# Attention taken in natural tile order, low weights in one transfer per chunk, small softmax steps on ACT, late weights over two superblocks

## The chip, the cores and the metric

The kernel runs on one core of a Trainium2 chip. The time is that of one execution on the device, in microseconds (us). The engines are TensorE (PE; PEld is its weight load), VectorE (DVE), ScalarE (ACT), GpSimd (POOL) and SyncE (SP), which here issues nearly all transfers. Each engine runs its own queue of instructions in order; engines wait for one another by semaphores.

## The reference

Three layers follow one another; `x` between them has 4608 tokens of 512 values.

```python
# attention, q, k, v: 8 batches x 8 heads x 576 x 64, in chunks of 64 positions
scores = scale * np.matmul(q_c, k_c.transpose(0, 1, 2, 4, 3))
scores = scores - np.max(scores, axis=-1, keepdims=True)
attn = np.exp(scores)
attn = attn / (np.sum(attn, axis=-1, keepdims=True) + 1e-09)
out = np.matmul(attn, v_c)
# layer 1 and layer 2 (512 -> 1536 -> 512); layer 2 takes xn
g = x @ w_gate
silu = g * (1.0 / (1.0 + np.exp(-g)))
val = x @ w_val
return (silu * val @ w_out).astype(np.float32)
# ahead of layer 2
rms = np.sqrt(np.mean(x * x, axis=-1, keepdims=True) + 1e-06)
xn = x / rms * rms_g
```

The weights come as float64 and are used to float32 accuracy.

## The kernel before

**Arithmetic.** Every float32 operand of a large product is split into a high part in a reduced type and a low part, and each product is three matmuls (`mm3`, L570 to L572): high x high, low x high, high x low. A weight thus exists as a high tile (kept on the chip) and a low tile.

**Stages of layer 1.** Seven blocks of 512 tokens (numbered 0 to 6), each in 12 chunks of the hidden size; a chunk has 36 matmuls of 128x512: 12 for g, 12 for v, 12 for y of the chunk before. Block 0 (26 to 143 us of the trace, "the head") also turns the float64 weights into high and low parts on ACT and VectorE: L124, L125, L135, L140, and `to_lo` (L158), which computes a low tile; `keep` (L1271) stores it to `lo_scratch` five conversions later. From block 1 on (143 us) `load_lo` (L179, transfer at L182) loads the low tiles of g, v and o of a chunk, two chunks ahead, into three sets of buffers. Between the blocks' matmuls stand, one attention tile (128 tokens) every 6.75 positions with three positions to a chunk: 28 tiles (8 to 35) lie in blocks 1 to 5, so each block has 5 or 6 of them and block 6 has none. `load_qk` and `load_v` make lists of transfers for groups of five chunks of 64 tokens; `issue` (L376, L378) issues them on SyncE, a few at a time.

**Attention tile.** `trans_att` transposes q and k, TensorE computes the scores (L406), `att_m` takes the maximum on VectorE (L426), scales it on POOL (L429), and ACT makes the exponentials `p` and their sums `r` (L434); `att_n` adds 1e-9 to `r` on POOL (L454), VectorE inverts it (L463), POOL multiplies (L464), VectorE transposes (`att_td`, L480), and TensorE multiplies with v (L522). Which tokens tile i has is set by `order`: the layers' blocks hold natural token ranges, and tiles 28 to 35 (the last 1024 tokens) are taken in between others.

**Work beside it in blocks 0 to 5.** Weights of layer 2 are converted, combined (`comb_add`, L210) and split (`comb_split`, L216 to L218) on ACT and POOL and stored to `w_scratch`. For the last 1024 tokens layer 1 uses seven combined products per 2x2 blocks in place of eight, and its combined weights are made here: `whole` (L226, plain parts stored at L230), `first_add` (L245), `first_keep` (L248), with two buffers `wa`. All of these are placed by `put` at positions of blocks.

**Superblocks.** Superblock 0 (1043 to 1267 us) is layer 1 for the last 1024 tokens: 504 matmuls for g and v, 252 for y. Its combined weights come back from `w_scratch` whole and are split here by `ring_split` (ACT copy L870, POOL subtraction L871; 72 of them); the norm of block 6 (`rms_*`) and four late output weights of layer 2 (`late_o`, for fp 2 to 5) are placed among its matmuls by `late`. Superblocks 1 to 5 (1267 to 2057 us) are layer 2; in superblock 1 lies the norm of the last tokens (`norm`).

## Time and profile before

| | us |
|---|---|
| median of 3 runs | 2056.97 (2056.14 to 2058.54) |
| profiled execution | 2057.85 |
| its span in the trace | 2056.1 |

| engine | busy in us | share of the span |
|---|---|---|
| TensorE matmuls | 1795.0 | 87% |
| weight loads | 1485.1 | 72% |
| VectorE | 1283.3 | 62% |
| ACT | 802.3 | 39% |
| POOL | 607.6 | 30% |

The busy shares are a mean over stages with different limits, so they don't say what ends a stage. The trace is read by stage: a window gives the busy time of each engine in a stretch; a list of waits names who waited for whom; the chain goes back from the last instruction to what released it; the timeline gives single events. SyncE's issues are no busy time of an engine, but they take time in its queue and stand in the chain as SPq. All times below are from the one profiled execution.

### The profile page before, as it was taken

To read this page: it belongs to the slowest core of one execution; us is meant where nothing else is said; L and a number is where in the kernel's file an instruction comes from. 1 tells how busy PE (TensorE), PEld (TensorE's weight loads), DVE (VectorE), ACT (ScalarE), POOL (GpSimd) and SP (SyncE) were. 2 spreads that over 40 slices of the span, in tenths; PEclk is the share of its full clock that TensorE was granted. 3 is DMA by queue.
4 is the path that set the end of the run, shared out by engine and by line. 5 is a ranking of instruction groups with operands and counts; after the bars stand their busy time and mean duration, and the time that the engine had idled before them with its cause. 6 is when DMAs were issued, how large, how long until landed. Compare 5 with 4: busy or idle time off the path is not lost.

```text
span 2056.1 us, 30283 instructions
## 1 busy us (share of the span) xinstructions
PE 1795.0 (87%) x9978; PEld 1485.1 (72%) x9978; DVE 1283.3 (62%) x2208; ACT 802.3 (39%) x1846; POOL 607.6 (30%) x641
## 2 busy tenths in 40 slices
PE   7996587788476696799988899999999999999998
PEld 5875365566354575578876677778888888899998
DVE  7964265465254465576565596679558747758657
ACT  6751233332132142343344464335235334435333
POOL 1003245333444443453164665302001101101100
PEclk9998799899787898899999999999999999999999
DMA  9964455645554465663556636676876876797986
GB/s 246 299 167 114 116 169 156 178 137 141 140 161 139 108 192 160 171 192 114 159 168 201 219 114 191 181 243 198 251 214 182 267 209 189 212 321 223 325 252 188
DMA packets 489355, 391.11 MB, mean 190 GB/s; under 512 B 285424, under 2 KB 355312, under 8 KB 489200
## 3 DMA queue, kind: packets, MB, share of 16 engines
q1 hardware_dynamic: 487600, 388.99, 64.9%
q8 instruction: 80, 1.31, 0.3%
q14 instruction: 75, 0.61, 0.1%
q10 hardware_dynamic: 1600, 0.20, 0.1%
HBM read 309.07 MB, written 79.95 MB: 189 GB/s over the span
## 4 chain that ended last, share of the span: by engine, by line
PE 49%; SPq 13%; DVE 10%; DMA 10%; POOL 7%; issue 7%; ACT 3%; POOLq 0%; ACTq 0%; DVEq 0%
SPq L378 10%; DMA lo<-lo_scratch 2%; PE g L570 1%; DVE hp L1047 1%; PE g L571 1%; PE ygA L571 1%; PE g L572 1%; PE yvA L570 1%; PE yvA L572 1%; PE ygA L572 1%; PE yvA L571 1%; PE ygA L570 1%; ACT p L434 1%; DVE pT L480 1%; PE v L570 1%
## 5 line engine op out<-in xcount | busy, mean ns | idle before, releaser
L1011 POOL TENSOR_TENSOR h<-h,h 128x512 f32<-128x512 f32 (+1 forms) x36 | 46.4, 1290 | 510.6 <-DVE h L989 509.8
L572 PE MATMUL g<-xh,lg 128*128 128x512 f32 x336 | 139.6, 415 | 40.7 <-DMA lg<-lo_scratch 40.6
L570 PE MATMUL g<-xh,wg 128*128 128x512 f32 x336 | 140.8, 419 | 27.4 <-DVE sg L583 25.7
L1047 DVE TENSOR_TENSOR hp<-h,hp 128x512 fp32r<-128x512 f32 (+1 forms) x216 | 151.0, 728 | 6.6 <-ACT hp L1046 6.3
L570 PE MATMUL v<-xh,wv 128*128 128x512 f32 x336 | 135.4, 403 | 19.9 <-DVE sg L599 16.7
L480 DVE STREAM_TRANSPOSE pT<-p 32x128 f32<-32x128 f32 x448 | 135.6, 303 | 16.3 <-POOL p L464 10.1
L1046 ACT CAST hp<-h 128x512 fp32r<-128x512 f32 (+1 forms) x216 | 121.9, 584 | 57.3 <-PE yvA L572 21.0
L570 PE MATMUL y<-hh,wo 128*128 128x512 f32 x168 | 73.8, 439 | 76.8 <-ACT hh L602 76.8
L571 PE MATMUL g<-xl,wg 128*128 128x512 f32 x336 | 137.7, 410 | 0.4 <-DVE xl L564 0.4
L969 ACT ACTIVATE sig<-sgt 128x512 f32<-128x512 f32 (+1 forms) x108 | 64.5, 597 | 175.6 <-DVE sgt L977 175.6
L970 DVE TENSOR_TENSOR sgt<-sgt,sig 128x512 f32<-128x512 f32 (+1 forms) x108 | 72.3, 669 | 96.2 <-ACT sig L969 96.2
L571 PE MATMUL v<-xl,wv 128*128 128x512 f32 x336 | 132.0, 393 | 0.0
L572 PE MATMUL v<-xh,lv 128*128 128x512 f32 x336 | 131.8, 392 | 0.0
L908 POOL TENSOR_TENSOR xf<-xf,xf 128x512 f32<-128x512 f32 (+1 forms) x48 | 80.0, 1666 | 156.7 <-DMA wro<-w_scratch 94.8
L602 ACT CAST hh<-sg 128x512 fp32r<-128x512 f32 x84 | 52.4, 624 | 149.2 <-DVE sg L599 149.1
L572 PEld LDWEIGHTS g<-xh,lg 128*128 128x128 f32 x336 | 67.4, 201 | 59.7 <-DMA lg<-lo_scratch 44.5
L463 DVE RECIPROCAL r<-r 128x8 f32<-128x8 f32 x36 | 7.3, 203 | 153.1 <-POOL r L454 152.9
L570 PEld LDWEIGHTS g<-xh,wg 128*128 128x128 f32 x336 | 67.4, 200 | 48.3 <-DVE sg L583 32.0
L571 PE MATMUL y<-hl,wo 128*128 128x512 f32 x168 | 74.6, 444 | 30.2 <-DVE hl L604 29.9
L434 ACT ACTIVATE p<-both,m 128x64 f32<-128x64 f32 x224 | 66.9, 327 | 81.9 <-POOL m L429 81.9
L570 PEld LDWEIGHTS y<-hh,wo 128*128 128x128 f32 x168 | 34.1, 203 | 88.3 <-ACT hh L602 81.3
L583 DVE SCALAR_TENSOR_TENSOR sg<-sg,g 128x512 f32<-128x512 f32 x84 | 56.8, 676 | 56.8 <-ACT sg L582 56.4
(859 smaller groups left out, 5454.3 us busy)
## 6 DMA issues: line engine op xcount, KB each, us to landing
wrg<-w_scratch SPq DMA_DIRECT2D x210, 256.0 KB, 3.3
wrv<-w_scratch SPq DMA_DIRECT2D x210, 256.0 KB, 3.3
wro<-w_scratch SPq DMA_DIRECT2D x210, 256.0 KB, 3.1
lg<-lo_scratch SPq DMA_DIRECT2D x54, 256.0 KB, 3.0
lv<-lo_scratch SPq DMA_DIRECT2D x54, 256.0 KB, 3.4
lo<-lo_scratch SPq DMA_DIRECT2D x54, 256.0 KB, 3.7
w_scratch<-wsg SPq DMA_DIRECT2D x42, 256.0 KB, 2.4
w_scratch<-wsv SPq DMA_DIRECT2D x42, 256.0 KB, 2.3
```

Of the source, the lines that this page charges most:

```text
L378: nc.sync.dma_start(out=o, in_=i)
L434: nc.scalar.activation(pt[:, hp, x], s3[:, x, hp], AF.Exp, scale=SCALE, bias=m[:, x, hp:hp + 1], accum_out=r[:, 2 * hp + x],)
L480: nc.vector.transpose(out=pT[o:o + 32, :, r:r + 32], in_=pt[r:r + 32, :, z, b * 32:b * 32 + 32])
L570: nc.tensor.matmul(o, sh, mh, start=first, stop=False, skip_group_check=free)
L571: nc.tensor.matmul(o, sh, ml, start=False, stop=False, skip_group_check=free)
L572: nc.tensor.matmul(o, sl, mh, start=False, stop=last, skip_group_check=free)
L583: return sg, lambda: nc.vector.scalar_tensor_tensor(out=sg[:, :n], in0=sg[:, :n], scalar=1.0, in1=g[:, :n], op0=ALU.add, op1=ALU.mult)
L908: nc.gpsimd.tensor_sub(o, a, b)
L969: nc.scalar.activation(sg[:, :tw], src[:, :tw], AF.Sigmoid)
L970: nc.vector.tensor_mul(t[:, :tw], src[:, :tw], sg[:, :tw])
L1046: nc.scalar.copy(hh[:, :tw], src)
L1047: nc.vector.tensor_sub(hl[:, :tw], src, hh[:, :tw].bitcast(F32))
```

## The change

- **Order and storage.** Attention tiles go through the tokens in natural order. Which columns of the layers' storage a tile takes is set by `home` and `order`: tiles 33, 34, 35, 12, 13, 22, 23 and 24 are the last 1024 columns. A group of five chunks is then a continuous range, except where a batch ends, so its q and k come in fewer, wider transfers: 832 before, 544 after. Stores of the result follow `rows`: 172 in place of 156, the 16 more in the last superblock.
- **Low weights.** The low tiles of g, v and o of a chunk are one tile and one transfer of 768 KB (L184 of the new kernel), 54 in place of 162. The tile's buffer is released when its last reader is done.
- **Stores of combined weights** go in pairs: 72 in place of 126.
- **Small softmax steps.** The scaling of the maximum (L449) and the 1e-9 (L456) are ACT's for tiles 8 to 35; POOL's two are gone.
- **`ring_split`.** VectorE subtracts 34 of the 72 and the low halves of the others stay on POOL.
- **Late weights.** `late_o` for fp 2 and 3 stays in superblock 0, at positions 30 and 50; for fp 4 and 5 it goes to superblock 1, at positions 3 and 23.

SyncE's transfers in the two programs, counted in the order of its queue from the load of a chunk's low weights to the next (chunks 3 to 10 one by one; the last number is chunk 11 with chunks 0 to 2 of the next block):

| block | before | after |
|---|---|---|
| 1 | 22, 48, 44, 24, 18, 7, 3, 7, 99: 272 | 10, 31, 28, 18, 14, 4, 1, 5, 61: 172 |
| 2 | 28, 34, 22, 18, 10, 7, 3, 35, 83: 240 | 26, 31, 20, 15, 7, 4, 1, 18, 51: 173 |
| 3 | 52, 50, 12, 14, 11, 8, 24, 37, 101: 309 | 21, 19, 8, 11, 7, 5, 20, 34, 65: 190 |
| 4 | 49, 22, 13, 9, 8, 14, 33, 37, 88: 273 | 20, 12, 9, 6, 6, 12, 29, 34, 55: 183 |
| 5 | 21, 13, 5, 9, 8, 19, 19, 14, 24: 132 | 14, 10, 2, 6, 6, 16, 16, 11, 19: 100 |

SyncE, block 1, from the low weights of the sixth chunk (index 5) to those of the seventh; `x3` and `x4` are like transfers in a row. Before:

```order
L182 DMA lg_1_5_2221<-lo_scratch 128x512
L182 DMA lv_1_5_2223<-lo_scratch 128x512
L182 DMA lo_1_5_2225<-lo_scratch 128x512
L378 DMA xk_2123<-in_k_dram 32x6x32 x3
L378 DMA xk_2123<-in_k_dram 32x2x32 x4
L378 DMA xq_2122<-in_q_dram 32x2x32 x4
L378 DMA xq_2122<-in_q_dram 32x6x32 x4
L378 DMA xq_2122<-in_q_dram 32x2x32 x4
L378 DMA xk_2123<-in_k_dram 32x2x32 x4
L378 DMA xk_2123<-in_k_dram 32x6x32 x4
L378 DMA xk_2123<-in_k_dram 32x2x32 x4
L378 DMA xq_2122<-in_q_dram 32x2x32 x4
L378 DMA xq_2122<-in_q_dram 32x6x32 x4
L378 DMA xq_2122<-in_q_dram 32x2x32 x2
L182 DMA lg_1_6_2344<-lo_scratch 128x512
```

After:

```order
L184 DMA l_1_5_2140<-lo_scratch 128x1536
L398 DMA xk_2057<-in_k_dram 32x4x32
L398 DMA xk_2057<-in_k_dram 32x6x32 x4
L398 DMA xq_2056<-in_q_dram 32x4x32 x4
L398 DMA xq_2056<-in_q_dram 32x6x32 x4
L398 DMA xk_2057<-in_k_dram 32x4x32 x4
L398 DMA xk_2057<-in_k_dram 32x6x32 x4
L398 DMA xq_2056<-in_q_dram 32x4x32 x4
L398 DMA xq_2056<-in_q_dram 32x6x32 x2
L184 DMA l_1_6_2245<-lo_scratch 128x1536
```

Between the loads of low weights stood 41 transfers of q and k pieces, most of them 2 wide, and now 27 of 4 and 6; the low weights are one row in place of three.

POOL, end of block 3, where the weights of chunk 10 are made whole (`wav`, third tile in two buffers). Before:

```order
L429 TENSOR_SCALAR m_5969<-m_5969 128x8
L226 TENSOR_TENSOR wav_5986<-wv_0_520,lv_3_10_5676 128x512
L245 TENSOR_TENSOR wav_5845<-wav_5845 128x256
L454 TENSOR_SCALAR r_5972<-r_5972 128x8
L464 TENSOR_TENSOR p_5970<-p_5970,r_5972 128x512
```

After:

```order
L228 TENSOR_TENSOR wav_5631<-wv_0_518,l_3_10_5330 128x512
L248 TENSOR_TENSOR wav_5491<-wav_5491 128x256
L480 TENSOR_TENSOR p_5614<-p_5614,r_5616 128x512
L228 TENSOR_TENSOR wav_5711<-wv_0_447,l_3_11_5449 128x512
L248 TENSOR_TENSOR wav_5631<-wav_5631 128x256
```

The small steps on `m` and `r` are gone from the row; `p` still comes after `wav`.

ACT at the scores of tile 24 (`both` is the scores, `wsv` a layer-2 weight, `hh` the hidden values of block 4, chunk 0). Before:

```order
L538 COPY x_23_6167<-both_6134 128x2x4x64
L434 ACTIVATE p_6211,r_6213<-both_6134,m_6210 128x64 x8
L216 CAST wsv_3_6237<-wtv_3_6185 128x256
L602 CAST hh_4_0_6207<-sg_4_0_6132 128x512
```

After:

```order
L554 COPY x_23_5808<-both_5775 128x2x4x64
L449 ACTIVATE m_5841<-m_5841 128x8
L452 ACTIVATE p_5842,r_5844<-both_5775,m_5841 128x64 x8
L456 ACTIVATE r_5844<-r_5844 128x8
L218 CAST wsv_3_5860<-wtv_3_5817 128x256
L618 CAST hh_4_0_5838<-sg_4_0_5773 128x512
```

Two steps of 128x8 stand around the exponentials, ahead of the weights' cast and of `hh`.

POOL in superblock 0 (`wrg`, `wrv` are low halves from `ring_split`, `lwt`, `lws` the late weights, `h` the hidden values). Before:

```order
L871 TENSOR_TENSOR wrg_4_0_10083<-wrg_4_0_10083 128x256
L1011 TENSOR_TENSOR h_1_0_10250<-h_1_0_10250,h_1_0_10094 128x512
L692 TENSOR_TENSOR ms_10102<-ms_10102,rr_10104 128x512
L217 TENSOR_TENSOR lws_0_10278<-lcr_10169,lws_0_10278 128x256
L217 TENSOR_TENSOR lws_0_10278<-lwt_10221,lws_0_10278 128x256
L871 TENSOR_TENSOR wrv_4_0_10097<-wrv_4_0_10097 128x256
L217 TENSOR_TENSOR lws_1_10299<-lcr_10193,lws_1_10299 128x256
L217 TENSOR_TENSOR lws_1_10299<-lwt_10221,lws_1_10299 128x256
L871 TENSOR_TENSOR wrg_3_0_10116<-wrg_3_0_10116 128x256
```

After:

```order
L1028 TENSOR_TENSOR h_0_0_9404<-h_0_0_9404,h_0_0_9270 128x512
L679 TENSOR_TENSOR al_9426<-acc_9287,ah_9425 128x512
L1028 TENSOR_TENSOR h_1_0_9602<-h_1_0_9602,h_1_0_9468 128x512
L708 TENSOR_TENSOR ms_9476<-ms_9476,rr_9478 128x512
L888 TENSOR_TENSOR wrv_5_0_9521<-wrv_5_0_9521 128x256
L212 TENSOR_TENSOR lwt_9749<-lcr_9702,lcr_9718 128x256
L212 TENSOR_TENSOR lwt_9749<-lwt_9749,lcr_9702 128x256
L888 TENSOR_TENSOR wrv_6_0_9579<-wrv_6_0_9579 128x256
```

The rows on `wrg` are no longer here (VectorE's queue has them), those on `wrv` are.

The diff:

```diff
--- before.py
+++ after.py
@@ -158,10 +158,11 @@
     def to_lo(nm, f):
         z = "gvo".index(nm)
         r, hi = made.pop((0, nm, f))
-        lo = wlo.tile([P, KD * P], F32R, tag=f"l{nm}{f % 3}", name=f"l{nm}_0_0_{f}")
-        wl_[0, 0, f, nm] = lo
+        if z == 0:
+            wl_[0, 0, f] = wlo.tile([P, 3, KD * P], F32R, tag=f"l{f % 3}", name=f"l_0_0_{f}")
+        lo = wl_[0, 0, f][:, z]
         nc.vector.tensor_sub(lo, r, hi.bitcast(F32))
-        keep.append((lo1_d[z, f], lo.bitcast(F32)))
+        keep.append((lo1_d[f, :, z], lo.bitcast(F32)))
 
     def chunk(j, f):
         return f if j % 2 == 0 else NF - 1 - f
@@ -174,13 +175,14 @@
     def low_of(l, j, f, nm):
         if j and f < 3:
             return low_of(l, j - 1, NF - 1 - f, nm)
-        return wl_[l, j, f, nm]
+        return wl_[l, j, f][:, "gvo".index(nm)]
 
     def load_lo(l, j, f):
-        for z, nm in enumerate("gvo" if f > 2 else ""):
-            t = wlo.tile([P, KD * P], F32R, tag=f"l{nm}{slot(j, f)}", name=f"l{nm}_{l}_{j}_{f}")
-            nc.sync.dma_start(out=t.bitcast(F32), in_=lo1_d[z, chunk(j, f)])
-            wl_[l, j, f, nm] = t
+        if f < 3:
+            return
+        t = wlo.tile([P, 3, KD * P], F32R, tag=f"l{slot(j, f)}", name=f"l_{l}_{j}_{f}")
+        nc.sync.dma_start(out=t.bitcast(F32), in_=lo1_d[chunk(j, f)])
+        wl_[l, j, f] = t
 
     flat = {}
     NP2 = NF // 2
@@ -225,11 +227,12 @@
         h = whi[0, nm, f]
         nc.gpsimd.tensor_add(t, h.bitcast(F32), low_of(0, j, chunk(j, f), nm).bitcast(F32))
         flat[0, nm, f] = t
-        for k, (which, c) in enumerate(PLAIN[nm]):
-            if which == side:
-                nc.sync.dma_start(
-                    out=w1_d["gvo".index(nm), p, :, k], in_=h.bitcast(F32)[:, c * HK:(c + 1) * HK]
-                )
+        ks = [(k, c) for k, (which, c) in enumerate(PLAIN[nm]) if which == side]
+        k, c, n = ks[0][0], ks[0][1], len(ks)
+        nc.sync.dma_start(
+            out=w1_d["gvo".index(nm), p, :, k:k + n],
+            in_=h.bitcast(F32)[:, c * HK:(c + n) * HK].rearrange("p (k f) -> p k f", k=n),
+        )
 
     def first_add(nm, p, which):
         if which == 3:
@@ -244,8 +247,14 @@
         }[which]
         nc.gpsimd.tensor_tensor(out=t[which], in0=a, in1=b, op=op)
 
-    def first_keep(nm, p, which):
-        nc.sync.dma_start(out=w1_d["gvo".index(nm), p, :, which], in_=comb[0, nm, p][which])
+    def first_keep(nm, p, side):
+        nc.sync.dma_start(
+            out=w1_d["gvo".index(nm), p, :, 3 + 2 * side:5 + 2 * side],
+            in_=flat[0, nm, 2 * p + side].rearrange("p (k f) -> p k f", k=2),
+        )
+
+    def place(nm, k):
+        return {3: 6, 5: 4 if nm == "o" else 5, 4: 3, 6: 5 if nm == "o" else 4}[k]
 
     def w_of(l, j, f, nm):
         return [t.rearrange("p (c f) -> p c f", c=KD) for t in (whi[l, nm, chunk(j, f)], low_of(l, j, f, nm))]
@@ -260,9 +269,20 @@
 
     NCH = NT // CH
     SC = S // CH
-    order = list(range(12)) + [28] + list(range(12, 16)) + [29] + list(range(16, 20)) + [30, 31]
-    order += list(range(20, 24)) + [32] + list(range(24, 28)) + [33, 34, 35]
-    assert sorted(order) == list(range(NT // P))
+    last = [33, 34, 35, 12, 13, 22, 23, 24]
+    home = [i for i in range(NT // P) if i not in last] + last
+    order = [home.index(i) for i in range(NT // P)]
+
+    def rows(t, n):
+        runs = []
+        for a in range(0, n, P):
+            i = home[(t + a) // P]
+            if runs and home[(t + a) // P - 1] == i - 1:
+                runs[-1][1] += P
+            else:
+                runs.append([a, P, i * P])
+        return runs
+
     EARLY = NW // P + 1
     groups = [list(range(0, 2 * EARLY - 2)), list(range(2 * EARLY - 2, 2 * EARLY))]
     while groups[-1][-1] + 1 < NCH:
@@ -274,7 +294,7 @@
     def segs_of(g):
         segs = []
         for n, z in enumerate(groups[g]):
-            c = 2 * order[z // 2] + z % 2
+            c = z
             if segs and segs[-1][2] == c // SC and segs[-1][3] + segs[-1][1] == c % SC:
                 segs[-1][1] += 1
             else:
@@ -426,15 +446,14 @@
         nc.vector.tensor_reduce(out=m, in_=s3, op=ALU.max, axis=AX.X)
         if i >= 8:
             r = att.tile([P, HP * 2, 1], F32, tag="r", bufs=2, name=f"r{i}")
-            nc.gpsimd.tensor_scalar(
-                out=m, in0=m, scalar1=-SCALE, scalar2=0.0, op0=ALU.mult, op1=ALU.add
-            )
+            nc.scalar.mul(m, m, -SCALE)
             for x in range(2):
                 for hp in range(HP):
                     nc.scalar.activation(
                         pt[:, hp, x], s3[:, x, hp], AF.Exp, scale=SCALE,
                         bias=m[:, x, hp:hp + 1], accum_out=r[:, 2 * hp + x],
                     )
+            nc.scalar.activation(r, r, AF.Copy, bias=1e-9)
             prob[i], rsum[i] = pt, r
             return
         nc.vector.tensor_tensor(
@@ -451,9 +470,6 @@
         p8 = pt.rearrange("p a b c -> p (a b) c")
         if i >= 8:
             r = rsum.pop(i)
-            nc.gpsimd.tensor_scalar(
-                out=r, in0=r, scalar1=1.0, scalar2=1e-9, op0=ALU.mult, op1=ALU.add
-            )
         else:
             r = att.tile([P, HP * 2, 1], F32, tag="r", bufs=2, name=f"r{i}")
             nc.vector.tensor_reduce(
@@ -811,7 +827,7 @@
         a = 3 * min(chunk(j, 2 * p), chunk(j, 2 * p + 1))
         for side in range(2):
             put(0, j, 3 * chunk(j, 2 * p + side), lambda nm=nm, j=j, p=p, side=side: whole(nm, j, p, side))
-        for d, (add, kept) in enumerate((((3,), ()), ((5, 4), (3,)), ((6,), (5, 4)), ((), (6,)))):
+        for d, (add, kept) in enumerate((((3,), ()), ((5, 4), ()), ((6,), (1,) if nm != "o" else ()), ((), (0,) if nm != "o" else (0, 1)))):
             for kk in add:
                 put(0, j, a + 4 + d, lambda nm=nm, p=p, kk=kk: first_add(nm, p, kk))
             for kk in kept:
@@ -848,12 +864,12 @@
             if s:
                 nc.sync.dma_start(out=t.bitcast(F32), in_=w2_d[z, fp, :, k])
             elif k > 2:
-                nc.sync.dma_start(out=t[:, 1].bitcast(F32), in_=w1_d[z, fp, :, k])
+                nc.sync.dma_start(out=t[:, 1].bitcast(F32), in_=w1_d[z, fp, :, place(m, k)])
             else:
                 side, c = PLAIN[m][k]
                 nc.sync.dma_start(out=t[:, 0].bitcast(F32), in_=w1_d[z, fp, :, k])
                 nc.sync.dma_start(
-                    out=t[:, 1].bitcast(F32), in_=lo1_d[z, 2 * fp + side, :, c * HK:(c + 1) * HK]
+                    out=t[:, 1].bitcast(F32), in_=lo1_d[2 * fp + side, :, z, c * HK:(c + 1) * HK]
                 )
             wt[s, m, fp, k] = t
             wnext += 1
@@ -868,7 +884,8 @@
             if s == 0 and k > 2:
                 t = wt[s, m, fp, k]
                 nc.scalar.copy(t[:, 0], t[:, 1].bitcast(F32))
-                nc.gpsimd.tensor_sub(t[:, 1], t[:, 1].bitcast(F32), t[:, 0].bitcast(F32))
+                eng = nc.gpsimd if wsn > 36 and m != "g" else nc.vector
+                eng.tensor_sub(t[:, 1], t[:, 1].bitcast(F32), t[:, 0].bitcast(F32))
 
     xo = {}
     xf = {}
@@ -1087,9 +1104,9 @@
         nc.vector.transpose(out=o[:, :tw], in_=src[:, :tw])
         i, j = int(pos[0]) - 1, int(pos[1]) - 1
         r0, c0 = t0 + j * tw, i * HK + q * P
-        for a in range(0, P, 32):
-            dst = out[r0:r0 + tw, c0 + a:c0 + a + 32].rearrange("(b t) d -> t b d", t=32)
-            src_ = o[a:a + 32, :tw].rearrange("t (b d) -> t b d", d=32)
+        for a, (x, n, r) in [(a, run) for a in range(0, P, 32) for run in rows(r0, tw)]:
+            dst = out[r:r + n, c0 + a:c0 + a + 32].rearrange("(b t) d -> t b d", t=32)
+            src_ = o[a:a + 32, x:x + n].rearrange("t (b d) -> t b d", d=32)
             queue = nc.scalar if s == len(SB) - 1 and pos == "12" and a >= 64 else nc.sync
             if slow:
                 held.append((dst, src_))
@@ -1401,10 +1418,11 @@
         late[28] = [lambda: rms_newton(pj)]
         for d in range(KD):
             late[30 + 2 * d] = [lambda d=d: rms_x(pj, d)]
+        norm = {}
         for fp in range(LATE, NP2):
+            first, z = divmod(fp - LATE, 2)
             for d, fn in enumerate(late_o(fp)):
-                late.setdefault(2 + 17 * (fp - LATE) + d, []).append(fn)
-        norm = {}
+                (norm if first else late).setdefault((3 if first else 30) + 20 * z + d, []).append(fn)
         for z in range(2):
             for d in range(KD):
                 norm.setdefault(2 + 2 * d + 8 * z, []).append(lambda z=z, d=d: tail_sq(z, d))
@@ -1516,7 +1534,7 @@
         with tc.tile_pool(name="dram", bufs=1, space=bass.MemoryType.DRAM) as dp:
             xn = dp.tile([512, 4608], F32, name="xn_scratch")
             w2 = dp.tile([3, 6, 128, 7, 2, 256], F32, name="w2_scratch")
-            lo1 = dp.tile([3, 12, 128, 512], F32, name="lo1_scratch")
+            lo1 = dp.tile([12, 128, 3, 512], F32, name="lo1_scratch")
             w1 = dp.tile([3, 6, 128, 7, 256], F32, name="w1_scratch")
             x1 = dp.tile([512, 1024], F32, name="x1_scratch")
             outs = []
```

## Rows read from the trace of the kernel before

**Rows 1.** Windows, head to superblock 1: stretch, length, PE, PEld, DVE, ACT, POOL busy, PEclk, DMA, GB/s
```profile
26.00:143.00 117.00, 109.81 (x724) 87.13 (x725) 102.44 (x169) 83.37 (x149) 5.99 (x5) 1.00 0.88 248
143.00:313.00 170.00, 122.08 (x789) 95.23 (x789) 77.68 (x167) 45.92 (x154) 52.17 (x65) 0.86 0.50 135
313.00:465.00 152.00, 120.53 (x753) 91.83 (x752) 85.02 (x175) 47.18 (x148) 62.30 (x76) 0.91 0.57 159
465.00:657.00 192.00, 119.99 (x757) 92.61 (x755) 86.98 (x176) 48.23 (x150) 77.25 (x92) 0.83 0.53 150
657.00:816.00 159.00, 121.06 (x820) 94.77 (x821) 84.57 (x173) 50.01 (x165) 61.42 (x76) 0.86 0.53 151
816.00:943.00 127.00, 110.58 (x756) 88.31 (x755) 85.58 (x174) 45.80 (x146) 66.88 (x79) 0.93 0.59 172
943.00:1043.00 100.00, 100.00 (x529) 82.38 (x528) 56.11 (x89) 30.16 (x63) 25.36 (x20) 1.00 0.46 148
1043.00:1267.00 224.00, 193.04 (x773) 150.33 (x772) 156.06 (x196) 115.41 (x249) 144.89 (x142) 0.94 0.55 174
1267.00:1439.00 172.00, 169.13 (x736) 138.69 (x735) 126.81 (x185) 73.76 (x127) 42.01 (x30) 0.99 0.70 206
```

**Rows 2.** Chain of waits, 165 to 262 us: start us, length us, what
```profile
179.73 3.96 DMA lo<-lo_scratch
...
258.43 0.79 PE both L522 x32
259.21 0.47 PE both L406 x32
```

**Rows 3.** The page's chain over the whole span, by engine and by line
```profile
PE 49%; SPq 13%; DVE 10%; DMA 10%; POOL 7%; issue 7%; ACT 3%; POOLq 0%; ACTq 0%; DVEq 0%
SPq L378 10%; DMA lo<-lo_scratch 2%; PE g L570 1%; DVE hp L1047 1%; PE g L571 1%; PE ygA L571 1%; PE g L572 1%; PE yvA L570 1%; PE yvA L572 1%; PE ygA L572 1%; PE yvA L571 1%; PE ygA L570 1%; ACT p L434 1%; DVE pT L480 1%; PE v L570 1%
```

**Rows 4.** SyncE's timeline, 178 to 240 us: start, length us, issue, times
```profile
178.63 0.54 SPq L182 DMA_DIRECT2D lg<-lo_scratch  x1
...
218.63 5.65 SPq L378 DMA_DIRECT2D xq<-in_q_dram  x12
```

**Rows 5.** Line L378 (q, k, v loads): issue to landing
```profile
DMA to landing us min/median/max: 1.5/2.0/9.7
```

**Rows 6.** Waits, 143 to 943 us: waiter <- releaser: us, times, longest
```profile
DVE r L463 <- POOL r L454: 150.9, 25, 30.0
...
PE y L570 <- ACT hh L602: 76.8, 11, 14.2
POOL wav L226 <- DMA w_scratch<-wav: 76.3, 7, 26.4
...
PE g L572 <- DMA lg<-lo_scratch: 40.6, 8, 9.9
```

**Rows 7.** Timeline, 636 to 650 us: start, length us, event [idle before <- releaser]
```profile
645.35 1.26 POOL L226 TENSOR_TENSOR wav<-wv,lv 128x512 f32<-128x512 f32 x1 [13.02 <-DMA w_scratch<-wav]
...
647.38 0.20 POOL L454 TENSOR_SCALAR r<-r 128x8 f32<-128x8 f32 x1
647.61 0.20 DVE L463 RECIPROCAL r<-r 128x8 f32<-128x8 f32 x1 [16.54 <-POOL r L454]
```

**Rows 8.** Line L1271 (stores of low weights in the head): issue to landing
```profile
DMA to landing us min/median/max: 2.0/4.9/7.2
```

**Rows 9.** The page's costliest groups: count | busy, mean ns | idle before, releaser
```profile
L1047 DVE TENSOR_TENSOR hp<-h,hp 128x512 fp32r<-128x512 f32 (+1 forms) x216 | 151.0, 728 | 6.6 <-ACT hp L1046 6.3
...
L434 ACT ACTIVATE p<-both,m 128x64 f32<-128x64 f32 x224 | 66.9, 327 | 81.9 <-POOL m L429 81.9
```

**Rows 10.** POOL's groups, 1043 to 1267 us: count | busy us, mean ns | idle before
```profile
L871 POOL TENSOR_TENSOR wrv<-wrv 128x256 fp32r<-128x256 f32 x24 | 21.2, 882 | 9.3 <-ACT wrv L870 9.3
...
L217 POOL TENSOR_TENSOR lws<-lwt,lws 128x256 fp32r<-128x256 f32 x16 | 13.2, 828 | 0.6 <-ACT lws L216 0.6
```

**Rows 11.** TensorE's waits, 1043 to 1267 us: us, times, longest
```profile
PE p2vA L572 <- POOL wrv L871: 3.8, 1, 3.8
```

## The prediction

> **What bounds the kernel now.** I read the windows by stage first, then the chain of waits, the waits inside the slow stage, and last SyncE's own row of events there.
>
> The windows put the slack in one place [rows 1]. Blocks 1 to 5 (143 to 943 us) take 170, 152, 192, 159 and 127 us; block 6 has the same 432 large matmuls, no attention, and takes 100 us with TensorE busy throughout. Attention puts about 1.26 us per tile on TensorE (its two groups of 32 small matmuls, 0.79 + 0.47 [rows 2]), and 27 tiles lie in these blocks. Bare, the five would take 5 x 100 + 27 x 1.26 = 534 us. They take 800: **266 us too many**. The second slack is superblock 0, 224 us against the 172 us that superblock 1 takes for the same 756 matmuls, with VectorE, ACT and POOL busy longer. The rest is near TensorE's limit (169 us busy of 172 in superblock 1).
>
> The chain of waits names the first slack: 13% of the span, about 267 us, is SyncE's issuing, and 10% is the q/k/v loads of L378 alone [rows 3]. SyncE's events show why. Twelve q issues take it 5.65 us: a **pitch of 0.47 us per transfer** [rows 4]. The piece lands 2.0 us after its issue at the median [rows 5], and the next issue does not wait for that. A chunk of 36 matmuls lasts 100/12 = 8.3 us, about 9.5 with attention, so SyncE fits some 20 transfers into one. The table of counts in the part on the change gives what it is asked for: chunks with 40 to 52, up to 101 in four chunks. What lies above 20 per chunk (80 per four) adds up to 77, 42, 104, 69 and 1 in blocks 1 to 5. The blocks' lengths stand in that order: 192, 170, 159, 152, 127 for 104, 77, 69, 42, 1. Altogether 293 x 0.47 = 138 us is **plain overflow**.
>
> The other 266 - 138 = 128 us is knock-on: SyncE's queue is in order, so write-backs stand behind the loads, and other engines' queues are in order behind these. POOL waits 76 us for the write-back of `wav`; behind it stands the small `r` step, for which VectorE waits 151 us; behind that stands VectorE's `sg`, then ACT's `hh` made from it, for which TensorE waits 77 us [rows 6]. One case is whole in the trace: POOL's `wav` at 645.35 had waited 13.0 us for a write, `r` starts 2 us later, and VectorE had sat 16.5 us idle [rows 7].
>
> **The change part by part.** The sum is made on the profiled execution, 2057.85 us (span 2056.1), 0.9 us above the median of 2056.97; I carry no correction for that.
>
> *Fewer transfers (natural order, one low-weight load, merged stores).* Blocks 1 to 5 go from 1226 SyncE transfers to 818. By the same count the part above 20 per chunk falls from 293 to 19 + 17 + 15 + 23 + 0 = 74, or 35 us: **103 us of overflow goes**. Of the knock-on, if it scales with the overflow, 128 x 35/138 = 32 stays and 96 goes; if none goes, 128 stays. The gain is 103 to 199 us. I take the middle, **-150**: nearer to neither end, because the waits for write-backs are partly a matter of order (in block 3 POOL's third `whole` still follows the second pair at the same place, and only two buffers exist), while most of the 151 us wait comes from lateness. Cross-check: across the five blocks, length against overflow rises from 127 at 1 to 192 at 104, 0.63 us per transfer. By that slope the 219 transfers are worth 138.
>
> One rule speaks against this term. The Trainium skill ("DMA: Bandwidth & Descriptors", section "Issuing engines are not separate DMA queues") says that the sequencer's time to initiate a transfer is "usually small relative to the DMA itself"; by it the term is near 0 and the sum 150 us higher. The trace agrees for one transfer (0.47 against 2.0 us [rows 4, 5]), but these stand hundreds in a row in one queue. This is rival D.
>
> *The low-weight load.* One 768 KB transfer replaces three, but its buffer is free only when y of three chunks back is done (and POOL's `whole` of that chunk, where there is one). That y ends one chunk (8.3 us) before g needs the new load; SyncE already waits at this place for `y_b` today, for the third of the three. The bound for landing: the three issued back to back at 178.63 had landed at 179.73 + 3.96 = 183.69, 5.1 us [rows 2, 4]. One is not slower than three by any row here. Margin 3 us, cost 0. Queued behind SyncE's wait are the q/k loads and write-backs, as now. Where SyncE is late by more than 3 us (the chunks with 26 to 34 transfers), the wait is part of the overflow above.
>
> *Head (26 to 143 us).* The merged tile makes VectorE's `to_lo` of g wait for the store of the low out-weights three chunks back, issued two conversions before, where it had been four. Conversions come every 117/36 = 3.25 us; stores land in 4.9 us at the median and 7.2 at most [rows 8]. Two of them are 6.5 us: most are in time, some late by about 1 us, for nine chunks. VectorE is busy 102 of 117 us [rows 1], so what it loses shows: behind `to_lo` stand the next conversion and the `sg` steps that TensorE's y needs. Ends: -5 (fewer q/k issues stand before the stores) and +21 (nine chunks, 7.2 - 4.9 each); I take **+5**.
>
> *Small softmax steps to ACT.* 28 of `m` and 28 of `r` leave POOL. On ACT one costs between POOL's 0.20 us [rows 7] and the 0.33 us of a 128x64 exponential [rows 9]: 11 to 18 us in all, in blocks where ACT is busy 46 to 50 us each [rows 1]. ACT had waited 82 us for POOL's `m` [rows 9]; now it has only VectorE before it. `p` (L464) stays on POOL, so a late write-back still holds up `pT`. Behind the new ACT steps stand the low-part casts and `hh`; at 0.3 us each they are covered by ACT's idle time; the built order has no further table load. Cost 0, gain contained in the knock-on.
>
> *Superblock 0: splits to VectorE, late weights spread.* POOL is busy 145 of 224 us there [rows 1]. 34 subtractions of 0.9 us and about half of the late weights (22 operations of 0.83 us: 18 us) leave it [rows 10]: 49 us less. VectorE gains 34 x 0.36 to 0.73 us (half and whole of its 128x512 subtraction, L1047 [rows 9]), 12 to 25 us on 156 of 224. TensorE waits singly for such a subtraction, 3.8 us in one case [rows 11]. The stage is 224 - 172 = 52 us above superblock 1; ends 0 and -50. I take **-30**, since the norm of block 6 and the late weights' conversions still lie there.
>
> *Superblock 1 and the end.* The other half of the late weights lands here: some 20 us for POOL (busy 42 of 172), but TensorE is busy 169 of 172 [rows 1], so nothing can be hidden that delays it: 0 to +12, taken **+4**. Sixteen more stores of the last superblock are 7.5 us of issue, under matmuls that follow: **+1**.
>
> **Sum:** 2057.85 - 150 + 5 - 30 + 4 + 1 = 1887.85, so **1888 us**. Its own range: the large term from -103 to -199 and superblock 0 from 0 to -50 are not both at one end; 1840 to 1935.
>
> **The rivals.**
> A. *Only the overflow goes.* The order of POOL's queue and two `wa` buffers keep the whole knock-on: -103, and superblock 0 gives nothing because VectorE takes up what POOL loses: 2057.85 - 103 + 5 + 4 + 1 = 1965. For it: `p` still stands behind `whole` on POOL. Against it: 25 of the waits for `r` are gone with the step itself.
> B. *All lateness goes.* Below 20 transfers in nearly all chunks there is no backlog to be late in: -199 to -231 (103 + 128), and -45 in superblock 0: 2057.85 + 5 + 5 - 45 less that, 1792 to 1824. For it: blocks 5 and 6, where overflow is 1 or 0, lose little.
> C. *Slower: the low weights arrive late.* Every chunk then waits for the merged load. It decides from a landing of 8.3 us after the release; 54 loads, so each microsecond beyond costs 54 us, and all other gains (about 170) are eaten at 8.3 + 3.2 = 11.5 us. At 11.7 us: 1888 + 3.4 x 54 = 2072. Today TensorE waits 41 us for `lg`, eight times, behind SyncE's backlog [rows 6]. Against it: 5.1 us for the same bytes.
> D. *Issuing is not the bound.* If the pieces' landing sets the pace, wider pieces with the same bytes arrive no sooner, and the large term drops out: 2057.85 + 5 - 30 + 4 + 1 = 2038. For it: landing is four times the pitch. Against it: the chain shows issue after issue in L378 [rows 3] and the blocks' lengths follow the counts.
>
> **How the numbers follow.** Forecast 0.60; A 0.18; B 0.12; C 0.05; D 0.04; no change (gains given back exactly) 0.01. The predicted time is the forecast's, 1888. The range leaves out C, D and the outer half of B: 1808 to 1970. About 0.2% is what a measurement can tell from no change. Faster: forecast, A, B and D, 0.94; same 0.01; slower 0.05.
>
> **What would show it.** In the trace of the changed kernel: block 3 falls most, block 5 least; VectorE's wait for `r` on POOL is gone, and ACT's for `m` names VectorE; SyncE's share of the chain falls from 13% to below 5%; TensorE's waits for the low weights stay under 40 us. Wrong would be: blocks 1 to 4 still above 150 us (A or D; under A POOL waits for write-backs, under D TensorE's chain shows landings of q/k), TensorE waiting for `l` in most chunks (C), VectorE waiting for a store at L164 of the head by more than 20 us, or superblock 0 unchanged with VectorE as the one waited for.

## The result

The changed kernel takes 1926.38 us (median of 4 runs, 1924.93 to 1927.81), the kernel before 2056.84 beside it: a ratio of 0.9365 (95% interval 0.9348 to 0.9381). That is 130 us faster; 1888 was predicted, with a range of 1808 to 1970.

The windows of the changed kernel, from block 0 (the head) to superblock 1, stand beside [rows 1]. Columns: stretch, length, then busy time of PE, PEld, DVE, ACT and POOL, the granted clock, DMA share, GB/s.

```profile
25.00:151.40 126.40, 113.72 (x725) 89.39 (x726) 103.58 (x169) 84.20 (x149) 6.93 (x5) 0.97 0.88 244
151.40:284.50 133.10, 115.85 (x788) 91.81 (x787) 80.06 (x167) 48.66 (x167) 49.10 (x53) 0.92 0.62 167
284.50:417.50 133.00, 115.23 (x756) 90.37 (x755) 84.71 (x176) 48.97 (x158) 60.66 (x66) 0.94 0.65 178
417.50:574.90 157.40, 113.68 (x755) 89.77 (x754) 87.95 (x176) 50.53 (x160) 77.05 (x82) 0.88 0.63 178
574.90:701.30 126.40, 110.29 (x820) 88.14 (x819) 82.33 (x172) 52.03 (x176) 57.38 (x63) 0.95 0.69 193
701.30:814.90 113.60, 107.59 (x755) 85.67 (x754) 84.55 (x173) 47.92 (x156) 65.06 (x69) 1.00 0.63 188
814.90:915.50 100.60, 100.60 (x531) 82.89 (x530) 56.59 (x90) 30.96 (x65) 25.16 (x19) 1.00 0.44 147
915.50:1120.00 204.50, 186.18 (x772) 147.20 (x771) 158.54 (x221) 106.36 (x226) 95.68 (x85) 0.97 0.52 162
1120.00:1311.00 191.00, 179.75 (x761) 145.10 (x760) 138.87 (x202) 82.81 (x150) 61.49 (x53) 0.97 0.72 225
```

With the stage borders taken at the first matmul of each stage, the two profiled executions compare so (us):

| | start | head | block 1 | 2 | 3 | 4 | 5 | 6 | superblock 0 | 1 | 2 to 5 and end | span |
|---|---|---|---|---|---|---|---|---|---|---|---|---|
| before | 25.9 | 117.2 | 169.5 | 152.6 | 191.8 | 158.8 | 126.8 | 100.6 | 223.8 | 177.8 | 611.4 | 2056.1 |
| after | 25.0 | 126.4 | 133.1 | 133.0 | 157.5 | 126.4 | 113.6 | 100.6 | 204.5 | 191.1 | 613.8 | 1924.9 |
| difference | -0.9 | +9.2 | -36.4 | -19.6 | -34.3 | -32.4 | -13.2 | 0 | -19.3 | +13.3 | +2.4 | -131.2 |

(In [rows 1] superblock 1 was cut at 1439 us; by its border, 1444.7, it is 177.8.) Blocks 1 to 5 give 136 us, superblock 0 gives 19, and head, superblock 1 and end take 25 back.

The page's chain of waits over the whole span, to be read beside [rows 3]: SyncE's issuing is down from 13% to 4%. What comes next in the list is a store that [rows 3] did not have, `lo_scratch<-l`.

```profile
PE 55%; DMA 13%; DVE 12%; POOL 7%; issue 6%; SPq 4%; ACT 3%; DVEq 0%; POOLq 0%; ACTq 0%
DMA lo_scratch<-l 3%; SPq L398 3%; DVE pT L496 3%; PE v L586 2%; DMA l<-lo_scratch 1%; PE g L586 1%; PE v L588 1%; PE v L587 1%; PE g L588 1%; PE g L587 1%; ACT p L452 1%; PE ygA L587 1%; PE yvA L588 1%; PE ygA L588 1%; PE yvA L586 1%
```

Waits in blocks 1 to 5 of the changed kernel (151 to 815 us), beside [rows 6]: waiter, releaser, us in total, times, longest. VectorE's 151 us for `r` on POOL are now 47 on ACT, and TensorE's for the low weights are 15 instead of 41. POOL's wait for the write-back of `wav` is 43 us instead of 76.

```profile
DVE r L479 <- ACT r L456: 47.1, 22, 3.6
...
POOL wav L228 <- DMA w_scratch<-wav: 43.4, 5, 16.0
...
ACT m L449 <- DVE m L446: 29.3, 17, 4.5
...
PE g L588 <- DMA l<-lo_scratch: 15.1, 4, 5.2
```

### The profile page after: what moved, and what is told of

It is laid out like the page before. It is cut to its first block, busy times and chain, and to the rows that moved or that the text cites. A ratio compares the mean times of both kernels' runs of the same rounds, so it can differ in the third digit from the quotient of the medians.

```text
span 1924.9 us, 29765 instructions
## 1 busy us (share of the span) xinstructions
PE 1765.0 (92%) x9978; PEld 1468.4 (76%) x9978; DVE 1293.9 (67%) x2242; ACT 813.9 (42%) x1902; POOL 567.1 (29%) x551
## 4 chain that ended last, share of the span: by engine, by line
PE 55%; DMA 13%; DVE 12%; POOL 7%; issue 6%; SPq 4%; ACT 3%; DVEq 0%; POOLq 0%; ACTq 0%
DMA lo_scratch<-l 3%; SPq L398 3%; DVE pT L496 3%; PE v L586 2%; DMA l<-lo_scratch 1%; PE g L586 1%; PE v L588 1%; PE v L587 1%; PE g L588 1%; PE g L587 1%; ACT p L452 1%; PE ygA L587 1%; PE yvA L588 1%; PE ygA L588 1%; PE yvA L586 1%
## 5 line engine op out<-in xcount | busy, mean ns | idle before, releaser
L586 PE MATMUL g<-xh,wg 128*128 128x512 f32 x336 | 139.0, 414 | 36.1 <-DVE sg L599 34.3
L588 PE MATMUL g<-xh,l 128*128 128x512 f32 x336 | 136.5, 406 | 15.1 <-DMA l<-lo_scratch 15.1
L588 PE MATMUL v<-xh,l 128*128 128x512 f32 x336 | 131.8, 392 | 0.0
L480 POOL TENSOR_TENSOR p<-p,r 128x512 f32<-128x512 f32 x36 | 39.7, 1102 | 225.2 <-DVE r L479 181.4
L587 PE MATMUL y<-hl,wo 128*128 128x512 f32 x168 | 69.7, 415 | 28.6 <-DVE hl L620 28.2
L588 PEld LDWEIGHTS g<-xh,l 128*128 128x128 f32 x336 | 65.9, 196 | 32.1 <-DMA l<-lo_scratch 17.2
L586 PE MATMUL y<-hh,wo 128*128 128x512 f32 x168 | 69.0, 411 | 20.5 <-ACT hh L618 20.5
L598 ACT ACTIVATE sg<-g 128x512 f32<-128x512 f32 x84 | 50.0, 596 | 89.3 <-PE g L588 89.2
L586 PEld LDWEIGHTS v<-xh,wv 128*128 128x128 f32 x336 | 63.7, 190 | 24.0 <-DVE sg L615 7.2
```

The source lines that it names most:

```text
L586: nc.tensor.matmul(o, sh, mh, start=first, stop=False, skip_group_check=free)
L587: nc.tensor.matmul(o, sh, ml, start=False, stop=False, skip_group_check=free)
L588: nc.tensor.matmul(o, sl, mh, start=False, stop=last, skip_group_check=free)
```

## Experiments: is it the number of transfers?

**The old order back.** `order` is the old list, storage is natural, all else is as changed.

```diff
-    last = [33, 34, 35, 12, 13, 22, 23, 24]
-    home = [i for i in range(NT // P) if i not in last] + last
-    order = [home.index(i) for i in range(NT // P)]
+    order = list(range(12)) + [28] + list(range(12, 16)) + [29] + ...
+    home = list(range(NT // P))
...
-            c = z
+            c = 2 * order[z // 2] + z % 2
```

> The changed kernel with the old order of the attention tiles and natural storage; all else as changed. q and k loads go back from 544 to 832, and the transfers above 20 per chunk (80 per four) in blocks 1 to 5 from 74 to 225. Theory (SyncE's issuing sets the pace there): the change took 136 us off these blocks for 219 transfers fewer above that mark, 0.62 us each, so 151 of them cost 94 us, time 2020 (1995 at the bare 0.47 us each, to 2035), the loss in blocks 1 to 4 and none in block 5. Rival (bytes and landing set the pace): the same bytes in more pieces cost nothing, under 1940.

It took 2033.0 us (2031.4 to 2035.8). Blocks 1 to 5 were 160.5, 151.9, 186.8, 151.0 and 125.9 us, 113 more than in the changed kernel. Every other stage stayed within 3 us of it. So the order is worth 107 us of the 130. But block 5 lost 12 us with no transfer above the mark, so "above 20 per chunk" is not a sharp border. What does fit is the plain count. Between the stage borders SyncE's queue has 72, 42, 80, 62 and 34 transfers more than in the changed kernel: 290 for 113 us, or 0.39 us each, and 0.36 to 0.45 in every block, block 5 included.

**The same order and bytes in more pieces.** This separates the number of transfers from the order of the work.

```diff
+        for o, m, b, s in [x for x in segs if x[1] > 2] if g > 1 else []:
+            if cuts[0]:
+                cuts[0] -= 1
+                i = segs.index([o, m, b, s])
+                segs[i:i + 1] = [[o, 2, b, s], [o + 2, m - 2, b, s + 2]]
```

> The changed kernel with order, storage and bytes as they are; only 256 more transfers, by cutting q and k pieces of more than two chunks of 64 into two, in the groups of blocks 1 to 3. Transfers above 20 per chunk: 62, 61, 64, 23, 0 instead of 19, 17, 15, 23, 0. Theory (issuing): +43, +44, +49 at 0.47 to 0.63 us each is 20 to 31 us in each of blocks 1, 2 and 3, nothing in 4 and 5, time 1990 to 2012. Rival (bytes and landing): no change, 1927 +- 5. Rival (the order of the work, not the count, gave the gain): no change either.

It took 2027.9 us (2023.5 to 2030.0), above what the theory expected and far above both rivals. The windows of its blocks 1 to 5:

```profile
159.70:320.80 161.10, 122.87 (x788) 95.66 (x788) 77.67 (x167) 48.25 (x166) 48.37 (x53) 0.87 0.49 137
320.80:485.20 164.40, 127.82 (x755) 97.83 (x754) 83.85 (x175) 49.02 (x158) 60.19 (x66) 0.87 0.55 150
485.20:672.30 187.10, 120.49 (x755) 93.31 (x755) 88.07 (x178) 50.63 (x160) 75.07 (x82) 0.83 0.54 153
672.30:799.60 127.30, 112.43 (x819) 89.10 (x818) 82.65 (x171) 51.93 (x176) 56.85 (x63) 0.95 0.69 192
799.60:913.20 113.60, 107.59 (x755) 85.68 (x754) 84.58 (x174) 47.82 (x156) 65.01 (x69) 1.00 0.63 188
```

Blocks 1, 2 and 3, where pieces were cut, lost 28, 31 and 30 us; blocks 4 and 5, where none were, lost 1 and 0. The head lost 8; 25 of the 256 added transfers start there. Between the borders of blocks 1, 2 and 3 the queue has 76, 77 and 77 more: 89 us for 230 transfers, 0.39 us each, the price that the old order had, and some four fifths of the pitch of 0.47 [rows 4]. The same bytes moved, DMA's share fell, and the loads of q, k and v landed no later (2.3 us after their issue at the median, against 3.0 in the changed kernel). **This shows the cause of the large term: the number of issues on SyncE, not bytes, landing or order of work.** Rival D falls. Not all of the 89 us is waiting. TensorE's own busy time in the three blocks is 371 us instead of 345, at a granted clock of 0.83 to 0.87 instead of 0.88 to 0.94. Of the waits, TensorE's for the low weights grew from 13 to 38 us there; their loads stand in the same queue as the pieces.

The Trainium skill's sentence on it ("DMA: Bandwidth & Descriptors", section "Issuing engines are not separate DMA queues": the time to initiate a transfer is "usually small relative to the DMA itself") holds for one transfer here (0.47 against 2.0 us [rows 4, 5]); for these blocks the measurement decides against it.

## Experiments: what else in blocks 1 to 5?

**Three loads for the low weights.** Tiles and loads by g, v and o as before, in the new layout.

```diff
-        t = wlo.tile([P, 3, KD * P], F32R, tag=f"l{slot(j, f)}", name=f"l_{l}_{j}_{f}")
-        nc.sync.dma_start(out=t.bitcast(F32), in_=lo1_d[chunk(j, f)])
-        wl_[l, j, f] = t
+        for z, nm in enumerate("gvo" if f > 2 else ""):
+            t = wlo.tile([P, KD * P], F32R, tag=f"l{nm}{slot(j, f)}", name=f"l{nm}_{l}_{j}_{f}")
+            nc.sync.dma_start(out=t.bitcast(F32), in_=lo1_d[chunk(j, f), :, z])
+            wl_[l, j, f, nm] = t
```

> The changed kernel with the low weights of a chunk again in three tiles and three transfers of 256 KB. Transfers above 20 per chunk go from 74 to 97. Theory: blocks 1 to 5 lose 23 x 0.62 = 14 us; the head gets back the 8 us that VectorE's wait for the stores of low weights costs; net 1932 (1925 to 1942). Rival (the one large transfer lands late and holds up TensorE): the blocks gain instead, 1905 to 1920.

It took 1912.9 us (1910.5 to 1916.8), so undoing this part made the kernel faster. Its head is back at 117 us, and blocks 1 to 5 take 663.9 us against 663.5. The head's window, and blocks 1 and 5:

```profile
25.80:142.90 117.10, 110.17 (x724) 87.25 (x725) 102.93 (x169) 83.57 (x149) 6.42 (x5) 1.00 0.90 247
142.90:281.20 138.30, 118.24 (x788) 93.25 (x787) 80.22 (x167) 49.01 (x168) 49.95 (x54) 0.90 0.64 176
...
696.70:806.80 110.10, 106.50 (x756) 85.89 (x755) 85.23 (x173) 48.08 (x156) 65.09 (x69) 1.00 0.66 195
```

Block 1 loses 5 us and block 5 gains 3.5. The 90 issues that the merge saves in these blocks buy nothing that shows in sum (in three kernels of the next section that leave these blocks as changed, they take 662 to 669 us). What the count left out is SyncE's waits. In blocks 1 to 5, first of the changed kernel:

```profile
SPq L184 <- PE y_b L588: 84.7, 24, 10.3
...
SPq L398 <- DMA l<-lo_scratch: 21.2, 22, 2.0
```

and of this one:

```profile
SPq L182 <- PE y_b L586: 64.8, 18, 9.1
...
SPq L396 <- DMA lo<-lo_scratch: 1.8, 5, 0.6
```

The merged load stops SyncE's queue until the last reader of all three tiles, `y_b`, is done. With three loads those of g and v go out ahead of that, and only the third waits for it. The queue stops in either kernel; with fewer issues SyncE waits 20 us more in total for this release, and 19 us more at q, k and v loads that the list shows waiting for a merged load to land. Together that is 39 us, against the 42 us that 90 issues take at 0.47. That this is what eats the 90 issues is read from these rows; no run separates it.

**Small softmax steps back on POOL.**

```diff
-            nc.scalar.mul(m, m, -SCALE)
+            nc.gpsimd.tensor_scalar(
+                out=m, in0=m, scalar1=-SCALE, scalar2=0.0, op0=ALU.mult, op1=ALU.add
+            )
...
-            nc.scalar.activation(r, r, AF.Copy, bias=1e-9)
```

> The changed kernel with the scaling of the maximum and the 1e-9 of tiles 8 to 35 on POOL again; all else as changed. Theory: on POOL they stand behind its waits for write-backs (in the changed kernel 43 us for wav and 80 us for wsg and wsv in blocks 1 to 5), so blocks 1 to 5 lose 10 to 40 us: 1937 to 1967, block 3 most. Rival (p stands on POOL behind the same waits anyway, so nothing is saved by moving two small steps): 1922 to 1932.

It took 1947.8 us (1946.1 to 1948.4): the move is worth 21 us, 15 of them in block 3. The wait that looked so large is back almost whole, in blocks 1 to 5:

```profile
DVE r L483 <- POOL r L474: 139.9, 25, 17.6
```

On ACT the same wait is 47 us, so 93 us of VectorE's wait in the list stood for 24 us of time in these blocks. The rest did not make them longer.

**The multiplication by `r` on VectorE.** No step of attention is then POOL's.

```diff
-        nc.gpsimd.tensor_tensor(
+        (nc.vector if i >= 8 else nc.gpsimd).tensor_tensor(
             out=p8, in0=p8, in1=r.to_broadcast([P, HP * 2, CH]), op=ALU.mult
```

> The changed kernel with the multiplication of the exponentials by r (tiles 8 to 35) on VectorE instead of POOL, so that no step of attention is POOL's. Theory (what is left in block 3 is POOL's queue: p stands behind a wav that waits for its write-back, TensorE waits 42 us in block 3 for what follows): block 3 falls by 20 to 35 us, blocks 1, 2, 4, 5 by 0 to 8 each: 1865 to 1905. Rival (VectorE is the tighter engine, 28 x 0.7 = 19 us more on it): 1925 to 1945.

It took 1911.6 us (1906.7 to 1914.3). Block 3 fell by 15.5 us, less than expected, and block 4 rose by 6.5. The direction was right, the size was not.

**A third buffer for the combined weights.**

```diff
-        t = cv.tile([P, KD * P], F32, tag="wa", bufs=2, name=f"wa{nm}{f}")
+        t = cv.tile([P, KD * P], F32, tag="wa", bufs=3, name=f"wa{nm}{f}")
```

> The changed kernel with three buffers wa in place of two for the combined weights of layer 1; nothing else. Theory (POOL waits for a buffer until its write-back has gone out behind SyncE's loads): the wait of 43 us shrinks to under 15 and block 3 falls by 12 to 30 us: 1897 to 1915. Rival (the writes are late by more than one buffer covers, since they stand in SyncE's queue): POOL waits one tile later, 1920 to 1928.

It took 1901.2 us (1896.8 to 1906.1), 25 less. Block 3 alone went from 157.4 to 132.4, the other stages stayed within some 3 us:

```profile
411.90:544.30 132.40, 111.39 (x755) 87.64 (x753) 85.33 (x176) 49.22 (x158) 72.32 (x78) 0.94 0.70 197
```

POOL's wait for the write-back in block 3 halved, where less than 15 us had been expected. The list for 412 to 545 us:

```profile
POOL wav L228 <- DMA w_scratch<-wav: 20.6, 4, 9.3
```

In the changed kernel it was 43.4 us, all of it in block 3 (417.5 to 575 us):

```profile
POOL wav L228 <- DMA w_scratch<-wav: 43.4, 5, 16.0
DVE pT L496 <- POOL p L480: 27.6, 5, 15.2
...
PE g L586 <- DVE sg L599: 21.8, 4, 14.7
```

There the knock-on that rival A named was real, and it was a matter of buffers: POOL waits, `p` waits behind it, then VectorE's `pT` and `sg`, then TensorE. The run shows what the buffer is worth; the order of the steps is read from these rows.

**Single stores.** The combined weights stored one by one as before, 126 transfers instead of 72, by `first_keep` for each piece:

```diff
-    def first_keep(nm, p, side):
+    def first_keep(nm, p, which):
+        nc.sync.dma_start(out=w1_d["gvo".index(nm), p, :, which], in_=comb[0, nm, p][which])
```

> The changed kernel with the combined weights of layer 1 stored one by one again, 126 transfers for 72; all else as changed. Transfers above 20 per chunk go from 74 to 85. Theory (count): 11 x 0.65 = 7 us in blocks 1 to 5, 1931 to 1938. Rival (an earlier store of each piece frees the buffer wa sooner, which POOL waits for in block 3): 1915 to 1925. The old single stores go out one to two positions earlier than the pairs.

It took 1931.4 us, but its four runs lie at 1924, 1928, 1935 and 1936. In the profiled one (1935.6) block 3 was 9 us longer. The median fits the theory, the spread does not exclude zero: 0 to 12 us in blocks 1 to 5, left open.

## Experiments: head and superblocks

**Earlier stores in the head.**

```diff
-            while len(keep) > (5 if z < len(w1) else 0):
+            while len(keep) > (3 if z < len(w1) else 0):
```

> The changed kernel with the head's stores of low weights issued three conversions after the tile is made instead of five. Theory (the merged tile makes VectorE wait for the store of the out-weights three chunks back, 17 us in the trace, and it is on the chain): with two conversions (about 6 us) more, the wait goes and the head is 8 us shorter: 1918 (1916 to 1921). Rival (the transfers of the head, DMA share 0.88, are what is late): no change, 1925 to 1928.

It took 1919.2 us (1917.4 to 1926.1). VectorE's wait in the changed kernel's head (25 to 151 us),

```profile
DVE l L164 <- DMA lo_scratch<-l: 17.0, 6, 6.9
```

is no longer in this kernel's list, and its head takes 119.7 us:

```profile
25.10:144.80 119.70, 111.98 (x725) 88.40 (x726) 103.20 (x169) 83.63 (x149) 6.67 (x5) 0.99 0.90 252
```

The profiled execution is the slowest of the four, and its blocks 1 to 5 took 5 us more than those of the changed kernel, so the gain in the head hardly shows in its total; the other three took 1917 to 1919 us. The added wait is the head's loss. Its size varies: the changed kernel and the six others with the same head (those on small steps, `p`, buffers, splits, late weights and single stores) have 121.4 to 126.4 us there, the changed one's being the highest. Against 117.2 the cost is 4 to 9 us.

**All splits on POOL, and all late weights in superblock 0.** The change did two things for POOL in superblock 0; each is undone alone.

```diff
-                eng = nc.gpsimd if wsn > 36 and m != "g" else nc.vector
-                eng.tensor_sub(t[:, 1], t[:, 1].bitcast(F32), t[:, 0].bitcast(F32))
+                nc.gpsimd.tensor_sub(t[:, 1], t[:, 1].bitcast(F32), t[:, 0].bitcast(F32))
```

> The changed kernel with all 72 subtractions of superblock 0's weights on POOL again. Theory (POOL's load made superblock 0 long): POOL gets 31 us more there and superblock 0 goes from 204 to 212 to 220 us: 1935 to 1943. Rival (moving the late weights of fp 4 and 5 out is what shortened it): superblock 0 stays within 3 us, 1924 to 1930.

```diff
-            first, z = divmod(fp - LATE, 2)
             for d, fn in enumerate(late_o(fp)):
-                (norm if first else late).setdefault((3 if first else 30) + 20 * z + d, []).append(fn)
+                late.setdefault(2 + 17 * (fp - LATE) + d, []).append(fn)
```

> The changed kernel with all four late output weights in superblock 0 at their old positions (2, 19, 36, 53); the 34 subtractions stay on VectorE. Theory (with the subtractions back on POOL superblock 0 kept its 205 us, so the late weights' move alone shortened it, and superblock 1 pays for it): superblock 0 goes from 204 to 215 to 224 us, superblock 1 from 191 to 177 to 179; 1923 to 1934, so the move is worth 0 to 7 us. Rival (each of the two moves alone is enough to relieve POOL): superblock 0 stays within 4 us of 204 and superblock 1 gets its 13 us back: 1911 to 1917.

They took 1927.1 us (1924.2 to 1932.9) and 1925.7 us (1925.0 to 1927.6): neither part, undone alone, changes the whole. Both undone together were not run. Superblock 0 with the splits on POOL:

```profile
911.20:1116.60 205.40, 185.33 (x772) 147.44 (x771) 144.50 (x188) 106.98 (x226) 126.45 (x120) 0.97 0.52 162
```

and superblocks 0 and 1 with the late weights in superblock 0:

```profile
912.60:1132.00 219.40, 190.21 (x771) 147.96 (x770) 166.83 (x229) 115.54 (x248) 113.43 (x107) 0.95 0.57 178
1132.00:1309.80 177.80, 174.97 (x761) 143.44 (x760) 133.13 (x194) 74.34 (x128) 44.30 (x31) 0.99 0.71 209
```

POOL carries 31 us more in the first (126.45 against 95.68 us) and superblock 0 is 1 us longer, less than it differs between kernels with the same superblock (202.4 to 204.7). In the second, superblock 0 is 15 us longer and superblock 1 is 13 us shorter: the late work costs about the same wherever it stands. In superblock 1 of the changed kernel, TensorE's busy time for the same matmuls is 179.75 us at a granted clock of 0.97, here 174.97 at 0.99. So 5 of the 13 us are slower matmuls and the rest is idle time.

**The parts put together.** Three loads and three buffers.

> The changed kernel with the low weights in three tiles and loads and with three buffers wa. Theory (the two lie in different stages, the head and block 3, so they add): 1926.4 - 13.5 - 25 = 1888 (1883 to 1895). Rival (with 18 more issues in blocks the third buffer is worth less): 1896 to 1903.

It took 1886.7 us (1885.7 to 1890.3), a ratio of 0.918 to before (0.9168 to 0.9195). Head and block 3 add up as expected; blocks 1 to 5 take 632 us. This version beats both kernels.

**The same with late loads further ahead.**

```diff
             lambda: (load(f), load(g)),
-            lambda: None,
-            lambda: None,
+            *[lambda: None] * 5,
```

> The kernel with three loads and three buffers (1886.7 us), and each late output weight's work starts six positions after its load instead of three. Theory (of the 13 us that superblock 1 lost, the larger part is queues that stand behind an ACT step that waits for a load of 5 to 6 us, 6% of the chain there): superblocks 0 and 1 fall by 4 to 8 us each, 1871 to 1880. Rival (it is the late work itself on ACT, VectorE and POOL between the steps that TensorE needs): within 3 us, 1883 to 1890.

It took 1891.1 us (1883.9 to 1893.6): no gain. Superblock 0 fell from 204.0 to 200.6 us and superblock 1 rose from 191.1 to 192.7. ACT's wait for the load is gone from the list, and the time is not. The wait for the load was not what costs in superblock 1. That it is the work itself is what remains; it fits the 13 us that superblock 1 gained when all late weights stood in superblock 0, and was not shown directly.

## Why the prediction was right, and where not

- **The whole.** The profiled execution, 1927.03 us, is 39 us above the sum of 1887.85. Every term came out on the dear side: the blocks by 14 us, the head by 4, superblock 0 by 11, superblock 1 by 9 and the end by 1. The direction and the bound were right; the gains were put too high and the costs too low throughout.
- **The bound.** SyncE's issuing was the first slack, as the chain said: adding issues alone, with nothing else changed, brings 0.39 us back for each. For the q and k pieces the price goes by every transfer and not by those above 20 per chunk: the old order cost 0.36 us per transfer in block 5 too, where none lies above the mark. The transfers of the merged load bought nothing.
- **The large term, -150, measured -136.** The total came out, the working less so. It was split into 103 us of overflow and part of 128 us of knock-on, both tied to transfers above 20 per chunk. The runs give other parts: 113 us for the order, 24 for the small steps, 0 to 12 for the paired stores, 0 for the merged load; undone one at a time, 137 to 149. Without the small steps the change to the transfers is worth about 112 us (136 less 24), 38 less than the term. That the whole missed by 14 only is in part luck: the small steps, which the working gave nothing of their own, made up for 24. One step that failed is the count of the merged load among the transfers saved: 23 of the 219 above the mark are its, and they bought nothing. By the working's slope of 0.63 they were 14 us of the 150; that the miss has the same size proves nothing, since other parts were off as well. The working had assumed that SyncE's wait at the merged load costs nothing, because of a margin of 3 us.
- **Small steps: 0 of their own, measured 21.** They were counted as contained in the knock-on, and the step was mis-sized the other way: most of the 151 us wait was taken to be lateness that fewer transfers would cure. With fewer transfers and the steps on POOL it is 140 us still; with the steps on ACT it is 47, and these 93 us of wait are 24 us of time. The length of a wait in the list was a poor measure of either.
- **Block 3 and rival A.** The reason to take the middle and not all of the knock-on, two buffers and POOL's order in block 3, was right: block 3 stayed the longest, and one more buffer takes 25 us off it. Rival A as a whole (1965 us) falls, but what it gave the transfers, 103 us, is nearer to their 112 than the forecast's 150. B falls: blocks 1 to 4 keep some 20 to 52 us above the 105 or 106 that they need bare.
- **Head: +5, measured +9 in the profiled execution, 4 to 9 over all.** Step and mechanism right, the size small; 17 us of VectorE's wait came where two conversions had been argued to cover most.
- **Superblock 0: -30, measured -19; superblock 1: +4 (at most +12), measured +13.** This is the other step that failed. The busy time that leaves POOL was counted as gain; the 34 subtractions were worth 1 us once the late weights were gone, and the late weights took along as much as they gave. Forecast as -26 together, it is -6, and no part of that shows in the time when either is undone alone.
- **End: +1, measured +2.4.** With the old stores, in the run with the old order, the stretch was 611.8 us as before; the 16 stores cost 2 us.
- **Two readings of the trace before.** Block 6 is not without attention: of the 28 tiles 27 lie in blocks 1 to 5 and the last in block 6, where the attention's matmuls take TensorE 1.9 us. Bare, the five blocks thus need about 525 us and not 534, and their slack was 275 us. Superblock 1 was cut 5.7 us short: it takes 177.8 us and not 172, so superblock 0 stood 46 us above it and not 52. Neither changes which stage had the slack.
- **Rival C** (slower, a late merged load): the load landed in 4.9 us at the median and 7.1 at most, under the 8.3 from which it would have decided.

```profile
DMA to landing us min/median/max: 4.0/4.9/7.1
```

Of the signs named ahead, VectorE's wait for `r` on POOL is gone, ACT's for `m` names VectorE, SyncE's share of the chain is 4% and TensorE's wait for the low weights 15 us. Block 5 fell least, but block 1 fell most and not block 3, which at 157 us stayed above the 150 named as a sign of rival A and kept its wait for write-backs.

## What to carry to other kernels

Where one engine issues all transfers, count issues per stretch of the pipeline and price each by the pitch its timeline shows (here 0.39 of 0.47 us came out as time); cutting pieces in two without changing the bytes tests that price directly. Before merging transfers, look at what frees their buffers: a merged tile waits for its last reader, and its first writer for the last store. Read a long wait in the list, or busy time taken off an engine, as a place to test and not as a gain: here 93 us of wait were 24 us of time, and 31 us of POOL's work were 1.

## What was not expected of the hardware

One load of 768 KB landed in 4.9 us at the median, about what the three of 256 KB issued back to back had taken (5.1 us), so here nothing in the landing speaks for or against the merge. The clock followed the idle time: the 432 matmuls and the attention of block 3 ran at a granted clock of 0.88 with 157 us, and of 0.94 when a third buffer made it 132 us, so that 2.3 us of the 25 came from TensorE's own busy time.
